# A decode layer with cached attention and a gated MLP: hand-set semaphores and a TensorE loop in place of the tile framework, and another order of the first loads

## The chip, the cores and the metric

The program runs on one core of a Trainium2 chip. Five engines work side by side: TensorE (PE in the profile, its weight loads PEld), VectorE (DVE), ScalarE (ACT), GpSimd (POOL) and SyncE (SP, which here issues nearly all transfers). Data moves from HBM into SBUF through DMA; products are accumulated in PSUM. The metric is the device time of one execution in microseconds, the median of the runs.

## The reference

One new token for each of 8 sequences. All arrays are float32; B = 8, D = 512, 32 query heads, 8 heads of K and V, 4096 cached positions, head size 128.

```python
xn = _layernorm(x, axis=-1)
# A: attention over the cache, four query heads share one K/V head
q = (xn @ wq).reshape(B, Sq, Hq, Dh)
scores = jnp.einsum("bhqd,bhkd->bhqk", q, k) * (Dh ** -0.5)
p = _softmax(scores, axis=-1)
o = jnp.einsum("bhqk,bhkd->bhqd", p, v)
s = o.reshape(B, Sq, Hq * Dh) @ wo
# B: gated MLP on the same xn, F = 1792, Fh = 896
z = _gelu(xn @ w_in)
z1 = z[..., :Fh]
z2 = _layernorm(z[..., Fh:], axis=-1)
g = w_sp * z2 + b_sp
return x + s * _silu((z1 * g) @ w_out)
```

The caches are 8 x 8 x 4096 x 128 floats each, 134 MB for K and as much for V; wq and wo have 8.39 MB each, w_in 3.67 MB and w_out 1.84 MB. Everything is read once.

## The kernel before

**Buffers.** SBUF holds three slots of 64 KB in each of 128 partitions (8.39 MB each): `pair[0]` and `pair[1]`, called slot0 and slot1, and `side`. The two slots of the pair take turns: for each head h, the first four batches' K goes to slot0, the last four's to slot1, then V in the same way. `side` holds the MLP weights at first and wo at the end.

**Order of the loads**, all on SyncE's queue in program order: `w_mlp` (w_in and five of the seven 128-row blocks of w_out, L77), three small transfers `w_low` (L82: the other two blocks of w_out, cut into pieces of a few rows and laid on 20, 16 and 12 partitions, with outer sizes 5, 4 and 3), `wq` into slot1 (L92), K of head 0 first half into slot0 and, when the projection has read wq, second half into slot1 (L348). Each later load waits until its slot has been read: V (L355) until `scores` has read K, the next head's K until `values` has read V. In the last head wo comes into `side` (L359), 12 of its 32 pieces before the last V half and the rest behind it in ever smaller transfers. x (L72) comes in two transfers on ScalarE's queue.

**The work.** A float32 product is two matrix instructions with a weight load each. After the layer norm of x (L148 to L156) the generator `mlp` runs up to its `yield` (z, gelu, second norm, L185 to L218); then `project_q` twice (L269 to L279), which makes the 32 queries; then the rest of `mlp`: transposes (L222, L232), the product with w_out in 20 pieces, 15 of which are `w_low` pieces (L246), and the gate. Then the 8 heads one after another: `spread_q` (L286) copies the head's queries into a padded tile, `scores` (L293) multiplies them with a K half, `softmax` (L298 to L325) takes maxima, exponentials and sums over both halves and transposes the probabilities, `values` (L335) multiplies them with V for one batch; VectorE masks and folds the result (L338, L340), and `combine` (L344) adds it into `po_ps` one batch later. At the end come the product with wo (L366, L374), the gate, the sum with x, and the store (L432).

**What sets the order.** The tile framework writes all heads out one after another, puts a semaphore wait into each instruction that needs one, and closes the program (L470) with waits of SyncE for all counts, a barrier of all engines, a clearing of the semaphores and a second barrier. At the start there is one barrier (L466), which belongs to the program frame.

Of the kernel before, what the change touches and what calls it, by code (L numbers as in the profile page):

```python
# [1 line left out]

# [9 lines left out]
AX = mybir.AxisListType  # L12

# [13 lines left out]
UNIT = 2 * G * 512  # L27
SLOT = HALF * UNIT
# [4 lines left out]
LOW_R = 4  # L33
MAIN = [0, 2, 4, 6, 5]


def rows_of(j, lo, hi, n):
    return [(j, r) for r in range(lo, hi, n)]


LOW = [(5, 0, 0, rows_of(1, 0, 80, 20) + rows_of(3, 0, 100, 20)), (4, 0, 9 * D, [(3, 100)]),
       (3, R, 0, rows_of(1, 80, P, 12) + [(3, 116)])]
LOW_COLS = 10 * D
HL_AT = [0, 9, 0]
HL_CH = 10
X_PARTS = 2
ALIGN = 200
XW = D + 64
E = 2
W = P // E  # L50


@with_exitstack
def tile_gqa_gmlp_decode(ctx: ExitStack, tc: tile.TileContext, x, kT, v, wq, wo,
                         w_mlp, lows, out):
    nc = tc.nc
    const = ctx.enter_context(tc.tile_pool(name="const", bufs=1))
    ring = ctx.enter_context(tc.tile_pool(name="ring", bufs=1))
    work = ctx.enter_context(tc.tile_pool(name="work", bufs=1))
    small = ctx.enter_context(tc.tile_pool(name="small", bufs=2))  # L60
    ps_fix = ctx.enter_context(tc.tile_pool(name="ps_fix", bufs=1, space=bass.MemoryType.PSUM))
    ps = ctx.enter_context(tc.tile_pool(name="ps", bufs=2, space=bass.MemoryType.PSUM))

    const.tile([P, ALIGN], F32, name="align")

    side = ring.tile([P, SLOT], F32, name="side")
    pair = [ring.tile([P, SLOT], F32, name=f"slot{i}") for i in range(2)]


    xs_sb = work.tile([B, XW], F32, name="x_sb", tag="p")  # L70
    for c in range(0, XW, XW // X_PARTS):
        nc.scalar.dma_start(xs_sb[:, c:c + XW // X_PARTS], x[:, c:c + XW // X_PARTS])  # L72
    x_sb = xs_sb[:, :D]

    mlp_slot = side
    n_in, n_mlp = NK * 2 * FH, NK * 2 * FH + len(MAIN) * D
    nc.sync.dma_start(mlp_slot[:, :n_mlp], w_mlp)  # L77
    w_in_sb = mlp_slot[:, :n_in].rearrange("p (k n) -> p k n", k=NK)
    low_sb = []
    for (e, p0, c0, chunks), w_low in zip(LOW, lows):  # L80
        t = mlp_slot[p0:p0 + e * LOW_R, n_mlp + c0:n_mlp + c0 + len(chunks) * D]
        nc.sync.dma_start(t, w_low[:, :LOW_R * len(chunks) * D].rearrange("e (i n) -> e i n", i=LOW_R))  # L82
        low_sb.append(t.rearrange("p (c d) -> p c d", d=D))
    w_out_sb = mlp_slot[:, n_in:n_mlp].rearrange("p (j d) -> p j d", d=D)
    spare = [n_mlp + LOW_COLS]

    def from_slot(rows, n):
        lo = spare[0]
        spare[0] = lo + n
        return mlp_slot[:rows, lo:lo + n]  # L90

    nc.sync.dma_start(pair[1], wq)  # L92
    wq_sb = pair[1].rearrange("p (k n) -> p k n", k=NK)


    ident = const.tile([P, P], F32, name="ident")
    make_identity(nc, ident)
    neg_half = const.tile([P, 1], F32, name="neg_half")
    nc.gpsimd.memset(neg_half, -0.5)
    ones = const.tile([1, P], F32, name="ones")  # L100
    nc.gpsimd.memset(ones, 1.0)
    xnT = const.tile([P, NK, R], F32, name="xnT")
    nc.gpsimd.memset(xnT, 0.0)
    qT = const.tile([P, HKV, B, REP], F32, name="qT")
    qz = const.tile([P, B * (R + REP)], F32, name="qz")
    nc.gpsimd.memset(qz, 0.0)
    same = const.tile([P, G, R], F32, name="same")
    nc.vector.tensor_reduce(same[:, 0, :], ident.rearrange("p (g r) -> p r g", g=G),
                            op=ALU.add, axis=AX.X)
    for g in range(1, G):  # L110
        nc.vector.tensor_copy(same[:, g, :], same[:, 0, :])
    same_all = same.rearrange("p g r -> p (g r)")
    diag = const.tile([P, G], F32, name="diag")
    nc.vector.tensor_reduce(diag, same[:, 0, :G * REP].rearrange("p (g r) -> p g r", g=G),
                            op=ALU.add, axis=AX.X)
    fold = const.tile([P, REP], F32, name="fold")
    nc.vector.tensor_reduce(fold, same[:, 0, :G * REP].rearrange("p (g r) -> p r g", g=G),
                            op=ALU.add, axis=AX.X)

    same8 = const.tile([P, (E - 1) * B + R], F32, name="same8")  # L120
    nc.gpsimd.memset(same8, 0.0)
    nc.vector.tensor_copy(same8[:, (E - 1) * B:E * B], same[:, 0, :B])
    oT_end = const.tile([P, HKV * REP - FOLDED, (E - 1) * B + R], F32, name="oT_end")
    nc.gpsimd.memset(oT_end, 0.0)
# [5 lines left out]
    sc = ps_fix.tile([P, 2, 512], F32, name="sc")  # L130
    o_ps = [ps_fix.tile([P, G, DH], F32, name=f"o_ps{i}") for i in range(2)]
    po_ps = ps_fix.tile([P, 2, B * REP], F32, name="po_ps")
    for t in o_ps:
        nc.vector.memset(t, 0.0)

    def scratch(shape, name):
        t = ps.tile([P, 512], F32, name="scr")
        n = 1
        for s in shape[1:]:
            n *= s  # L140
        return t[:shape[0], :n]


    st = small.tile([B, 6], F32, name="st")
    mv = small.tile([B, 2], F32, name="mv")
    rstd = small.tile([B, 2], F32, name="rstd")
    xn = work.tile([B, D], F32, name="xn", tag="pT")
    nc.vector.bn_stats(st, x_sb)  # L148
    nc.vector.bn_aggr(mv, st)
    nc.vector.tensor_scalar(rstd[:, 0:1], mv[:, 1:2], EPS, None, op0=ALU.add)  # L150
    nc.gpsimd.tensor_tensor(rstd[:, 1:2], rstd[:, 0:1], neg_half[:B, 0:1], op=ALU.pow)
    nc.vector.tensor_scalar(xn, x_sb, mv[:, 0:1], rstd[:, 1:2], op0=ALU.subtract, op1=ALU.mult)  # L152
    pt = scratch([P, NK * B], "xnT")
    for k in range(NK):
        nc.tensor.transpose(pt[:, k * B:(k + 1) * B], xn[:, k * P:(k + 1) * P], ident[:B, :B])  # L155
    nc.vector.tensor_copy(xnT[:, :, :B], pt.rearrange("p (k b) -> p k b", k=NK))  # L156

    gate = const.tile([P, W], F32, name="gate")
    xg = const.tile([P, W], F32, name="xg")
    wb = const.tile([P, 2], F32, name="wb")  # L160
    px = scratch([P, W + 2], "px")
    for i in range(E):
        for g in range(G):
            lo = g * P + i * W
            nc.tensor.matmul(px[R * g:R * (g + 1), :W], shift(same8, i)[:B], x_sb[:, lo:lo + W],
                             start=(i == 0), stop=(i == E - 1))
    nc.tensor.matmul(px[:, W:], ones, xs_sb[0:1, D:D + 2], start=True, stop=True)
    nc.vector.tensor_copy(xg, px[:, :W])
    nc.vector.tensor_copy(wb, px[:, W:])

    def mlp():
        zu = work.tile([P, 4, FQ], F32, name="zu", tag="p")
        z, u = zu[:, :2], zu[:, 2:]
        hy = work.tile([P, 2 * D], F32, name="hy", tag="pT")
        hT = hy[:, :2 * P].rearrange("p (a s) -> p a s", a=2)
        hL = from_slot(P, HL_CH * P).rearrange("p (a s) -> p a s", s=P)
        y_sb, e = zu[:, :2].rearrange("p a f -> p (a f)"), zu[:, 2, :W]
        pz = scratch([P, 2 * FQ], "pz")
        nc.vector.memset(pz, 0.0)
        for part in range(2):  # L180
            for k in range(NK):
                for g in range(G):
                    lo = g * FQ
                    n = min(FQ, FH - lo)
                    nc.tensor.matmul(pz[R * g:R * (g + 1), part * FQ:part * FQ + n], xnT[:, k, :],  # L185
                                     w_in_sb[:, k, part * FH + lo:part * FH + lo + n],
                                     start=(k == 0), stop=(k == NK - 1))
        zf, uf = z.rearrange("p a f -> p (a f)"), u.rearrange("p a f -> p (a f)")
        nc.vector.tensor_copy(zf, pz)
        nc.vector.tensor_mul(uf, zf, zf)  # L190
        nc.vector.tensor_scalar(uf, uf, 0.044715, 1.0, op0=ALU.mult, op1=ALU.add)
        nc.vector.tensor_mul(uf, uf, zf)
        nc.scalar.activation(uf, uf, AF.Tanh, scale=GELU_C)
        nc.vector.tensor_scalar(uf, uf, 1.0, 0.5, op0=ALU.add, op1=ALU.mult)
        nc.vector.tensor_mul(zf, uf, zf)

        def mean(src, name):
            part_sum = small.tile([P, 1], F32, name="part_sum")
            nc.vector.tensor_reduce(part_sum, src, op=ALU.add, axis=AX.X)  # L199
# [25 lines left out]
        for (ne, p0, _, chunks), c0, w_low in zip(LOW, HL_AT, low_sb):  # L225
            n = ne * LOW_R
            for lo in range(0, len(chunks), 4):
# [5 lines left out]
                for i, (j, r) in enumerate(some):  # L233
                    if i and rows[i] == rows[0]:
                        continue
# [146 lines left out]
    for _ in steps:  # L382
        pass
# [92 lines left out]
```

## Time and profile before

| | |
|---|---|
| median of 3 runs | 687.27 us (686.05 to 687.49) |
| span of the profiled execution | 685.0 us |
| instructions in the profile | 5902, of them 2699 matrix products and 2699 weight loads |
| TensorE, VectorE, ScalarE busy | 56%, 25%, 2% |
| read from HBM | 290.74 MB, 424 GB/s over the span |
| granted TensorE clock, mean | 0.76 |

The profile records one execution on its own; the span runs from its first to its last instruction. Of that execution no time but the span is given; the runs' times were taken without the profiler. In the groups, "idle before" is the time that the engine stood still ahead of such instructions, with what ended it. In the chain, each piece is followed back to what released it; a piece named DMA runs from the issue of a transfer to its landing, so it also holds the time in which the transfer stood in the queue.

### The profile page before, as it was taken

What the parts mean: (1) busy time and instruction counts of PE and PEld (TensorE: products, weight loads), DVE (VectorE), ACT (ScalarE), POOL (GpSimd) and SP (SyncE); (2) the same over time, 40 slices, a digit from 0 to 9 for tenths busy, and PEclk for the clock granted to TensorE, in tenths of its full rate; (3) what the DMA queues carried; (4) which work ended last, traced back from release to release, by engine and by line L of the source; (5) the groups of instructions that cost most, each with busy time, mean ns of one, the idle gap of its engine ahead of it and who ended that gap; (6) DMA issues with size and microseconds to landing.
All of it is one profiled execution on the core that took longest, in us unless ns stands there. A gap on an engine that the chain in (4) does not pass through costs nothing.

```text
span 685.0 us, 5902 instructions
## 1 busy us (share of the span) xinstructions
PE 381.6 (56%) x2699; PEld 116.7 (17%) x2699; DVE 170.5 (25%) x284; ACT 13.4 (2%) x27; POOL 2.8 (0%) x14
## 2 busy tenths in 40 slices
PE   2268745556764464555755355555754465655656
PEld 1112111111211021111211021111211121111212
DVE  2413023401430024401421024401431024401432
ACT  0100000000000000000000000000000000000000
POOL 1000000000000000000000000000000000000000
PEclk9768967777787677767778777776687667767799
DMA  9999999999999999999999999999999999999996
GB/s 400 436 432 396 368 429 448 445 440 430 429 426 429 426 440 441 429 430 440 433 436 426 432 430 429 430 444 437 429 426 436 433 429 433 444 441 429 405 425 262
DMA packets 6308, 291.14 MB, mean 425 GB/s; under 512 B 844, under 2 KB 860, under 8 KB 1388
## 3 DMA queue, kind: packets, MB, share of 16 engines
q1 hardware_dynamic: 6252, 290.75, 98.6%
q8 instruction: 21, 0.34, 0.2%
q10 hardware_dynamic: 32, 0.02, 0.0%
q14 instruction: 3, 0.02, 0.0%
HBM read 290.74 MB, written 0.03 MB: 424 GB/s over the span
## 4 chain that ended last, share of the span: by engine, by line
DMA 73%; PE 24%; DVE 1%; SPq 0%; issue 0%
DMA slot<-in_v 29%; DMA slot<-in_kT 29%; PE sc L293 11%; DMA side<-in_wo 10%; PE o_ps L335 9%; DMA slot<-in_wq 5%; PE scr L269 1%; PE sc L246 1%; PE po_ps L344 1%; SPq L82 0%; DVE o_sb L340 0%; PE scr L232 0%; DVE o_all L338 0%; DVE q_sb L272 0%; PE scr L275 0%
## 5 line engine op out<-in xcount | busy, mean ns | idle before, releaser
L293 PE MATMUL sc<-slot,qz 128*32 128x512 f32 x1024 | 145.9, 733 | 123.2 <-DMA slot<-in_kT 123.2
L335 PE MATMUL o_ps<-slot,pT 128*16 128x512 f32 x1024 | 155.5, 751 | 83.3 <-DMA slot<-in_v 83.3
L338 DVE TENSOR_TENSOR o_all<-o_ps,diag 128x512 f32<-128x512 f32 x64 | 44.3, 692 | 163.4 <-PE o_ps L335 163.4
L298 DVE TENSOR_REDUCE nm<-sc 128x1 f32<-128x1024 f32 x8 | 9.8, 1225 | 266.3 <-PE sc L293 266.3
L293 PEld LDWEIGHTS sc<-slot,qz 128*32 128x32 f32 x1024 | 35.5, 132 | 227.0 <-DMA slot<-in_kT 131.1
L340 DVE TENSOR_REDUCE o_sb<-o_all 128x128 f32<-128x512 f32 x64 | 67.8, 1060 | 2.2
L335 PEld LDWEIGHTS o_ps<-slot,pT 128*16 128x16 f32 x1024 | 30.6, 114 | 168.4 <-issue 113.0
L344 PE MATMUL po_ps<-fold,o_sb 128*128 128x4 f32 x128 | 24.6, 263 | 24.0 <-DVE o_sb L340 23.8
L344 PEld LDWEIGHTS po_ps<-fold,o_sb 128*128 128x128 f32 x128 | 19.0, 188 | 68.6 <-DVE o_sb L340 67.7
L324 PE MATMUL scr<-ident,p 128*128 128x128 f32 x64 | 14.8, 410 | 10.7 <-DVE p L319 10.7
L300 ACT ACTIVATE p<-sc,nm 128x1024 f32<-128x1024 f32 x8 | 8.9, 1114 | 554.6 <-DVE qz L286 460.1
L269 PE MATMUL scr<-slot,xnT 128*32 128x512 f32 x64 | 10.2, 798 | 9.5 <-DMA slot<-in_wq 9.5
L324 PEld LDWEIGHTS scr<-ident,p 128*128 128x128 f32 x64 | 11.9, 213 | 11.1 <-issue 11.1
L325 DVE COPY pT<-scr 128x512 f32<-128x512 f32 x16 | 11.1, 692 | 10.8 <-PE scr L324 10.7
L303 PE MATMUL scr<-ident,nm 128*1 128x128 f32 x8 | 2.2, 270 | 10.8 <-DVE nm L298 10.8
L316 PE MATMUL scr<-wl,same 128*128 128x1 f32 x16 | 3.4, 284 | 6.2 <-DVE wl L314 6.2
L185 PE MATMUL scr<-side,xnT 128*32 128x256 f32 (+1 forms) x64 | 4.9, 442 | 3.1 <-DMA side<-in_w_mlp 3.1
L155 PE MATMUL scr<-ident,xn 8*128 8x8 f32 x4 | 0.6, 254 | 10.5 <-DVE xn L152 10.5
L246 PE MATMUL sc<-side 20*32 20x512 f32 (+2 forms) x30 | 5.7, 650 | 0.8 <-DVE zu L249 0.8
L319 DVE TENSOR_SCALAR p<-p,w 128x1024 f32<-128x1024 f32 x8 | 6.0, 753 | 0.3
L366 PE MATMUL sc<-side,oT 128*8 128x512 f32 x48 | 5.7, 593 | 0.3 <-DMA side<-in_wo 0.3
L201 PE MATMUL scr<-part_sum,same 128*128 128x1 f32 x4 | 1.1, 348 | 8.3 <-DVE part_sum L199 8.3
(99 smaller groups left out, 75.1 us busy)
## 6 DMA issues: line engine op xcount, KB each, us to landing
slot<-in_v SPq DMA_DIRECT2D x2, 4096.0 KB, 32.2
side<-in_w_mlp SPq DMA_DIRECT2D x1, 4864.0 KB, 14.5
side<-in_wo SPq DMA_DIRECT2D x1, 3072.0 KB, 36.9
side<-in_wo SPq DMA_DIRECT2D x1, 2048.0 KB, 43.0
side<-in_wo SPq DMA_DIRECT2D x1, 1280.0 KB
side<-in_wo SPq DMA_DIRECT2D x1, 768.0 KB
side<-in_wo SPq DMA_DIRECT2D x1, 512.0 KB
side<-in_wo SPq DMA_DIRECT2D x2, 256.0 KB, 31.9
```

The lines of the kernel that those rows point to most:

```text
L246: nc.tensor.matmul(sc[R * g:R * (g + 1), bank, :], lhsT, rhs, start=(i < G), stop=(i + G >= len(part)))
L269: nc.tensor.matmul(pq[R * g:R * (g + 1), :], xnT[:, k, :], wq_sb[:, k, lo:lo + REP * DH], start=(k == 0), stop=(k == NK - 1))
L293: nc.tensor.matmul(sc[R * g:R * (g + 1), c, :], qz[:, b * R:(b + 1) * R], k_sb[:, i, c, g, :], start=(b == 0), stop=(b == B - 1))
L298: nc.vector.tensor_reduce(m, sc, op=ALU.max, axis=AX.XY, negate=True)
L300: nc.scalar.activation(p.rearrange("p j s -> p (j s)"), sc.rearrange("p c s -> p (c s)"), AF.Exp, bias=m, accum_out=l[:, h:h + 1])
L319: nc.vector.tensor_scalar(p, p, w, None, op0=ALU.mult)
L324: nc.tensor.transpose(t[:, j * P:(j + 1) * P], p[:, 4 * c + j, :], ident)
L325: nc.vector.tensor_copy(pT[:, :, 4 * c:4 * c + 4].rearrange("p b j (g r) -> p (j g) b r", g=G), t.rearrange("p (m b r) -> p m b r", b=B, r ...
L335: nc.tensor.matmul(of[R * c:R * c + G * REP, :], pT[:, b, j, :], v_unit[:, j], start=(j < G), stop=(j >= J - G))
L338: nc.vector.tensor_mul(o_all, o, diag[:, :, None].to_broadcast([P, G, DH]))
L340: nc.vector.tensor_reduce(o_sb, o_all.rearrange("p g d -> p d g"), op=ALU.add, axis=AX.X)
L344: nc.tensor.matmul(po[:, b * REP:(b + 1) * REP], o_sb, fold, start=True, stop=True)
```

## The change

- The tile framework goes. A class `Program` takes a list of operations with the names of what each reads and writes, works out who must wait for whom, and gives each engine one semaphore and each slot one of its own. Waits are instructions of their own. SBUF addresses and PSUM banks are set by hand: three scratch banks, one bank for `po`.
- TensorE's instructions of heads 0 to 6 are emitted once, in a loop of seven passes. To make all passes alike, a wait inside the loop takes the awaited count off the semaphore. The other engines' instructions are written out as before. Head 7 follows behind the loop.
- The first loads are, in this order: wq, the MLP weights with all seven blocks of w_out in one transfer over 128 partitions, K of head 0. The three `w_low` transfers, the transposes that served them and 13 of the 20 products with w_out go.
- Both projections come ahead of the whole MLP; `spread_q` of the next head comes behind the softmax of the head before. x comes in one transfer.
- The program ends when SyncE has seen the output land; it clears the semaphores before that wait. There is no barrier and no drain.

```diff
+    def wait(self, eng, waits):
+        for s, n, take in waits:
+            w = self.eng[eng].wait_ge(self.sem(s), n)
+            if take:
+                w.then_inc(self.sem(s), -n)
+
+    def put(self, o):
+        eng = self.eng[o.eng]
+        self.wait(o.eng, o.waits)
+        ins = o.emit(eng)
+        if o.inc:
+            ins.then_inc(self.sem(o.inc[0]), o.inc[1])
+
+    def build(self):
+        self.settle()
+        self.assign()
+        for e in ("SP", "ACT", "DVE", "POOL"):
+            for o in self.ops:
+                if o.eng == e:
+                    self.put(o)
+        pe = [o for o in self.ops if o.eng == "PE"]
+        turns = [[o for o in pe if o.where == h] for h in range(LOOPED)]
...
+        with self.nc.Fori(0, LOOPED, engines=[ET.PE]):
+            for o in turns[0]:
+                self.put(o)
+        for o in pe[first + sum(map(len, turns)):]:
+            self.put(o)
...
-    nc.sync.dma_start(mlp_slot[:, :n_mlp], w_mlp)
-    w_in_sb = mlp_slot[:, :n_in].rearrange("p (k n) -> p k n", k=NK)
-    low_sb = []
-    for (e, p0, c0, chunks), w_low in zip(LOW, lows):
-        t = mlp_slot[p0:p0 + e * LOW_R, n_mlp + c0:n_mlp + c0 + len(chunks) * D]
-        nc.sync.dma_start(t, w_low[:, :LOW_R * len(chunks) * D].rearrange("e (i n) -> e i n", i=LOW_R))
...
-    nc.sync.dma_start(pair[1], wq)
+    n_in, n_mlp = NK * 2 * FH, NK * 2 * FH + NB * D
+    pr.dma(lambda e: e.dma_start(xs_sb, x), "x_in", writes=["x"], eng="ACT")
+    load(pair[1], wq, "slot1", ["slot1"])
+    load(side[:, :n_mlp], w_mlp, "mlp_in", ["side"])
...
+    project_q(0)
+    project_q(1)
...
+    load_k(0, 0)
+    load_k(0, 1)
...
+        for j in range(NB):
+            g = j % G
+            mm(sc[R * g:R * (g + 1), 0, :], hT[:, j % 2, R * (j // 2):R * (j // 2 + 1)], w_out_sb[:, j, :],
+               j < G, j + G >= NB, ["hT", "side"], ["sc"])
...
+    mlp()
...
-    steps = mlp()
-    next(steps)
-    project_q(0)
-    project_q(1)
-    for _ in steps:
-        pass
+    spread_q(0)
     for h in range(HKV):
         last = h == HKV - 1
-        spread_q(h)
+        pr.where = h if h < LOOPED else None
         for half in range(2):
-            scores(half, load_k(h, half))
...
+            if h:
+                load_k(h, half)
+        scores(0)
+        load(pair[0], v[h, 0], "slot0", ["slot0"])
+        scores(1)
...
+            load(pair[1], v[h, 1], "slot1", ["slot1"])
+        softmax(h)
+        if not last:
+            spread_q(h + 1)
...
+    pr.dma(lambda e: e.dma_start(out, res), "out", reads=["res"], writes=["out"])
+    pr.build()
...
+    for s in (range(used[0], done.num), range(done.num + 1, used[-1] + 1)):
+        if len(s):
+            nc.sync.sem_clear(s)
+    nc.sync.wait_ge(done, 16).then_inc(done, -16)
```

More of the change, by code (lines that the diff above doesn't have):

```diff
@@ L128, in shift @@
         return t[:, lo:lo + R]
[L130 to L161, printed above, removed]
+    px = scr[1]
     for i in range(E):
@@ L192, in mlp @@
[L192 to L199, printed above, removed]
-            pm = scratch([P, 1], "pm")
-            nc.tensor.matmul(pm, same_all, part_sum, start=True, stop=True)
-            t = small.tile([P, 1], F32, name=name)
-            nc.vector.tensor_scalar(t, pm, 1.0 / FH, None, op0=ALU.mult)
-            return t
@@ new lines, in values, with combine @@
+        t, u = o_all[b % 2], o_sb[b % 2]
+        dve(lambda e: e.tensor_mul(t, o, diag[:, :, None].to_broadcast([P, G, DH])),
+            [f"o_ps{b % 2}", "diag"], [f"o_all{b % 2}"])
+        dve(lambda e: e.tensor_reduce(u, t.rearrange("p g d -> p d g"), op=ALU.add, axis=AX.X),
+            [f"o_all{b % 2}"], [f"o_sb{b % 2}"])
+    def combine(b):
+        mm(po[:, b * REP:(b + 1) * REP], o_sb[b % 2], fold, True, True, [f"o_sb{b % 2}", "fold"], ["po"])
+    wo_sb = side.rearrange("p (m d) -> p m d", d=D)
@@ L387, in tile_gqa_gmlp_decode @@
         for half in range(2):
-            scores(half, load_k(h, half))
-        pT = softmax(h)
-        po = po_ps[:, h % 2]
+            if h:
[3 more added lines that the diff above has]
+        scores(1)
+        if last:
+            load_wo(0, 0, WO_EARLY)
+            for c in range(2):
+                n = SLOT // 2
+                load(pair[1][:, c * n:(c + 1) * n], v[h, 1][:, c * n:(c + 1) * n], f"v_end{c}",
+                     [f"v_end{c}"] + ([] if c else ["slot1"]))
+            for i, (lo, hi) in enumerate(WO_LATE):
+                load_wo(1 + i, lo, hi)
+        else:
+            load(pair[1], v[h, 1], "slot1", ["slot1"])
@@ L402, in tile_gqa_gmlp_decode @@
             for i in range(HALF):
                 b = half * HALF + i
-                o_sb = values(b, pT, v_sb[:, i])
+                key = f"slot{half}" if not (last and half) else f"v_end{i // 2}"
+                values(b, v_sb[:, i], key)
                 if b > 0:
-                    combine(b - 1, o_prev, po)
-                o_prev = o_sb
+                    combine(b - 1)
         if last:
             folded_wo(WO_EARLY, WO_LATE[0][1])
-        combine(B - 1, o_prev, po)
+        combine(B - 1)
@@ L469 @@
     out = nc.dram_tensor("out_0", (P, W), F32, kind="ExternalOutput").ap()
[L470 to L472 removed]
+    program(nc, *args, out)
+    nc.compile()
     r = run(nc, [{f"in_{name}": a for name, a in arrays.items()}], core_ids=[0])
```

580 lines of the change are left out of this document (325 added, 255 removed).

## The prediction

> **What bounds the kernel now.** I begin with the page: the busy times, the slices of the span, the DMA queues and the shares of the chain.
>
> ```profile
> PE 381.6 (56%) x2699; PEld 116.7 (17%) x2699; DVE 170.5 (25%) x284; ACT 13.4 (2%) x27; POOL 2.8 (0%) x14
> ...
> DMA  9999999999999999999999999999999999999996
> GB/s 400 436 432 396 368 429 448 445 440 430 429 426 429 426 440 441 429 430 440 433 436 426 432 430 429 430 444 437 429 426 436 433 429 433 444 441 429 405 425 262
> ...
> q1 hardware_dynamic: 6252, 290.75, 98.6%
> q8 instruction: 21, 0.34, 0.2%
> ...
> DMA 73%; PE 24%; DVE 1%; SPq 0%; issue 0%
> ```
>
> The reader is to see that all 16 DMA engines are busy in nearly every slice. One queue, q1, moves 290.75 MB and holds the engines 98.6% of the span. TensorE is busy 56%, but its 24% of the chain is no proof that it limits anything, as the chain in order of time and the waits show.
>
> ```profile
> 3.71 35.42 DMA slot<-in_wq
> ...
> 65.87 8.58 PE sc L293 x64
> ...
> 74.47 24.01 DMA slot<-in_v
> ...
> 108.86 28.32 DMA slot<-in_kT
> ...
> 137.22 8.85 PE sc L293 x64
> ...
> 146.09 29.80 DMA slot<-in_v
> ...
> 681.70 0.04 issue
> 681.75 0.47 PE sc L374 x16
> ```
>
> ```profile
> PE sc L293 <- DMA slot<-in_kT: 123.2, 15, 10.9
> PE o_ps L335 <- DMA slot<-in_v: 83.3, 17, 7.2
> ```
>
> A slot holds 8.39 MB. A load issued at 108.86 takes 28.32 us, though its bytes need only 19.4 us (rate in the next rows): for 9 us it stands behind the load of the other slot. TensorE in its turn waits for K 8.2 us a time (123.2 / 15). So in the steady part neither delays nor gains of under about 8 us on TensorE, VectorE or SyncE reach the end; DMA time alone counts. Where does it run below its rate?
>
> ```profile
> 0.00:2.00 2.00, 0.00 (x0) 0.00 (x0) 0.97 (x2) 0.00 (x0) 1.43 (x12) 1.00 0.78 219
> 2.00:4.00 2.00, 0.00 (x0) 0.00 (x0) 0.00 (x0) 0.00 (x0) 0.23 (x1) 1.00 0.55 195
> 72.50:75.00 2.50, 1.90 (x20) 0.36 (x12) 0.00 (x0) 0.00 (x0) 0.00 (x0) 1.00 0.37 157
> 100.00:640.00 540.00, 300.13 (x1984) 88.67 (x1976) 131.22 (x195) 9.86 (x21) 0.00 (x0) 0.74 1.00 433
> 640.00:675.00 35.00, 25.30 (x170) 6.88 (x174) 12.53 (x15) 0.00 (x0) 0.00 (x0) 0.82 0.99 424
> 677.00:679.00 2.00, 1.14 (x9) 0.12 (x9) 0.71 (x2) 0.00 (x0) 0.00 (x0) 1.00 0.70 281
> 679.00:681.00 2.00, 1.63 (x101) 1.50 (x104) 0.18 (x1) 0.00 (x0) 0.00 (x0) 1.00 0.25 97
> 681.00:683.00 2.00, 1.00 (x59) 0.68 (x47) 0.45 (x2) 0.00 (x0) 0.00 (x0) 1.00 0.04 13
> ```
>
> These are windows; the last two numbers are DMA share and GB/s. The steady rate is 433 GB/s. At it all bytes take 290.75 / 433 = 671.5 us. The first 4 us move 0.83 MB, worth 1.9 us, so the start costs 2.1 us. The small pieces of wo cost 35 x (1 - 424/433) = 0.7 us. A program with full and equal engines would thus land its last weights at 671.5 + 2.1 + 0.7 = **674.3 us**; this one lands them at 681.70. The 7.4 us between are what the change can reach:
> - a hole at 72.5: 2.5 x 0.63 = 1.6 us on every engine;
> - a ragged end: shares of 0.70, 0.25 and 0.04 mean that an average engine idles 0.6 + 1.5 + 0.7 = 2.8 us before 681.70, waiting for the last one;
> - the rest, 3.0 us, in which the instruction fetches are part: 0.2% of 685 us on 16 engines is 21.9 us, 1.04 us for each of 21, 1.4 us an engine.
>
> **The change part by part.** *wq first, MLP weights second.* The rows are SyncE's issues (the second number runs to the end of the last of them) and the first network's work.
>
> ```profile
> 1.18 2.49 SPq L82 DMA_DIRECT2D side<-in_w_low  x3
> 4.18 47.03 SPq L348 DMA_DIRECT2D slot<-in_kT  x2
> 74.47 10.86 SPq L355 DMA_DIRECT2D slot<-in_v  x2
> ```
>
> ```profile
> 15.32 4.89 PE L185 MATMUL scr<-side,xnT 128*32 128x256 f32 x64 [3.15 <-DMA side<-in_w_mlp]
> 20.28 0.69 DVE L189 COPY zu<-scr 128x512 f32<-128x512 f32 x1 [7.78 <-PE scr L185]
> 31.58 0.42 DVE L218 TENSOR_TENSOR zu<-zu 128x256 f32<-128x256 f32 x1
> 61.51 2.92 PE L246 MATMUL sc<-side 12*32 12x512 f32 x10 [0.82 <-DVE zu L249]
> ```
>
> Today the second K half is issued at 51.2, and `scores` of the first half begins at 65.87, after the last w_out product; so V is issued only at 74.47, when some engines have run dry: the hole. After: wq lands near 2.1 + 19.4 = 21.5; the projection (from wq's landing at 39.13 to the second K issue, 51.2 - 39.1 = 12.1 us) ends at 33.6 and frees slot 1, so the second K half is queued 20 us before the first ends (21.5 + 5.51 MB in 12.7 + 19.4 = 53.6). The MLP starts at 34.2: 4.9 us of products, 11.7 us from L189 to the end of L218, then w_out. That part takes 51.2 to 65.87 today, 14.7 us; 15 transposes, their copies and 13 of 20 products leave it, and I put 7 us, between 3 and 14.7. `scores` starts near 58 and takes 8.6 us; V is issued near 67, 6 us ahead of the second K half's end at 73. Gain: 1.6 us. Its cover is those 6 us; extra waits eat 1 to 2 of them. If it is gone, the 1.6 us come back.
>
> *w_low gone, w_out whole.* Three issues (2.49 us on SyncE) go; a full queue hides them either way. Their 0.52 MB stay, now in rows over all partitions. Where they lie today counts: by 39.13, when wq lands, 13.9 MB have passed, which take 32.1 + 2.1 = 34.2 us, so some engines are 4.9 us late. Per engine of five, four and three, the transfers of 360, 32 and 120 KB (by the code) are 72 + 8 + 40 = 120 KB, at 433 / 16 = 27 GB/s 4.5 us: the same delay. [...] With one transfer the engines start level.
>
> *TensorE's loop.* These groups make one head's instructions:
>
> ```profile
> L293 PE MATMUL sc<-slot,qz 128*32 128x512 f32 x1024 | 145.9, 733 | 123.2 <-DMA slot<-in_kT 123.2
> L335 PE MATMUL o_ps<-slot,pT 128*16 128x512 f32 x1024 | 155.5, 751 | 83.3 <-DMA slot<-in_v 83.3
> L344 PE MATMUL po_ps<-fold,o_sb 128*128 128x4 f32 x128 | 24.6, 263 | 24.0 <-DVE o_sb L340 23.8
> L324 PE MATMUL scr<-ident,p 128*128 128x128 f32 x64 | 14.8, 410 | 10.7 <-DVE p L319 10.7
> ```
>
> That is 2240 / 8 = 280 products a head, each with a weight load: 560 instructions and a few more. TensorE's 5398 make 257 per fetch of 16 KB, so the fetches follow its stream: 2.2 a head, 15 in heads 0 to 6. If a body once fetched is kept, six heads' 13 fetches vanish and 8 stay: 13 x 1.04 / 16 = 0.85 us for an average engine, more for the latest. The branch itself is not in this trace: at least nothing, at most a fetch that waits for its place; each pass ends where TensorE waits 8.2 us for K anyway, and I take 0.
>
> With engines level and 8 fetches left, what does the last engine carry beyond 674.3? At least nothing; from today's side, today's average end 681.70 - 2.8 = 678.9, less 1.6 and 0.85, is 676.4, plus one fetch 1.04: 677.5. Between 674.3 and 677.5 I take **676.6**, nearer to the end that is built from today's rows.
>
> *Own semaphores.* Waits become instructions of their own. Nearest rows are those of the closing part, by the timeline, the line's own instructions and the DMA issues:
>
> ```profile
> 682.75 0.34 SPq L432 DMA_DIRECT2D out<-res  x1
> ```
>
> ```profile
> L470 SPq EVENT_SEMAPHORE  x8: 17/27/28, 683.2 to 685.0; - x8
> ```
>
> ```profile
> out<-res SPq DMA_DIRECT2D x1, 32.0 KB, 1.5
> ```
>
> A wait holds SyncE for 17 to 28 ns; with its gap I put 0.06 us. Behind TensorE's waits stand the next products, behind VectorE's the two operations of each batch; some ten waits a half head are 0.6 us against 8 of slack. Only those after the last weights count: three or four, 0.2 us (bounds 0 and 0.4). `spread_q` moves behind the softmax of the head before, one small copy on VectorE, hidden by the 4.9 us (83.3 / 17) that TensorE waits for V. x comes in one DMA and is needed at 21.5. The PSUM banks are fixed by hand, three for scratch and one for `po` in place of two; po's copy has a whole head's time, and I count nothing.
>
> *No closing barrier.* The output is issued at 681.70 + 1.05 = 682.75 and lands 1.5 later, near 684.25; the span ends at 685.0, so nearly 0.8 us go. After: 676.6 + 1.05 + 1.5 + 0.2 = 679.35. That is **5.65 us** less than 685.0. The profiled execution has no time of its own beside its span; the median 687.27 stands 2.3 us above it. The profile does not show what lies there and I leave it: **681.6 us**.
>
> **The rivals.** (1) *The loop does not keep its body*: each pass brings its 2.2 to 3 blocks again. Fetches stay at 21 to 29, and the end stays ragged: average 678.9 - 1.6 = 677.3, plus up to 8 x 1.04 / 16 = 0.5, plus a lag of the last engine of 1.5 to 2.8 us: 678.8 to 680.6, and with 2.75 us behind it and 2.3 around it 683.85 to 685.65, middle **684.7**. For it: a fetch came for every 257 instructions, all new. Against: nothing shows that executed blocks are dropped. [...]
>
> (2) *Refetched through the same engine, slower*: if a block always comes by the same DMA engine, a pass adds its fetch there each time. It decides from the point at which one engine's load is 685.0 - 2.75 - 674.3 = 8.0 us above the even one, 1.1 us a pass over seven. One fetch is 1.04 us; with half of that again for the transfer it interrupts, 1.5 x 7 = 10.9, on 674.3 + 1.0 of other lag: 686.2 + 2.75 = 688.95, 3.95 us more than 685.0: **691.2**. For it: even fetching on all engines is nowhere shown. Against: it needs rival 1 and a fixed engine together.
>
> (3) *The hole stays*: the MLP now stands between the projection and `scores`; if it ends 6 us later than worked out, 1.6 us come back: **683.2**.
>
> **How the numbers follow.** Forecast 0.55, rival 1 0.24, rival 2 0.13, rival 3 0.08. The forecast's own range is 679.8 (last weights near 674.8) to 682.8 (677.5, and 0.4 us of waits); rival 3 lies at its edge, rival 1 reaches 685.65. Leaving out rival 2 and the far ends gives 679.8 to 685.8. What a measurement of this kernel can tell from no change is 0.2%, 1.4 us: faster means below 685.9. Forecast and rival 3 are faster (0.63), and two thirds of rival 1 (0.16), whose upper end all but touches the bound; its rest, 0.08, with 0.02 of rival 2, is the same: 0.79, 0.10 and 0.11.
>
> **What would show it.** Right: share near 1.0 between 66 and 80; q8 with about 8 packets; an end where the share falls from 0.9 to 0 within some 2 us; the last weights at 675 to 678; nothing behind the output's landing. Wrong: q8 with 21 packets or more (rivals 1 and 2; a last engine later than 681 tells 2), a share under 0.5 before 80 (rival 3), or TensorE's waits for K near zero, which would mean that the loop eats its slack.

## The result, and the profile after

The changed kernel takes 678.81 us (median of four runs, 678.80 to 680.64) against 686.67 us for the kernel before on the same chip: ratio 0.9891, 95% interval [0.9875, 0.9906]. That is 7.9 us; on a second chip (below, after_again) it was 678.51 against 686.08, 7.6 us. The forecast was 5.65 us and 681.6 us with a range from 679.8; the time came out 1.0 us under the range. The direction held, and so did most of the mechanisms; several sizes did not, and one part of the gain the forecast did not have at all.

The page of the kernel after, the slices of DMA and the queues:

```profile
DMA  9999999999999999999999999999999999999997
GB/s 380 441 434 435 433 433 427 433 433 433 437 433 433 433 437 433 433 433 433 433 433 434 433 433 434 433 433 433 433 433 433 433 433 433 433 433 434 422 432 326
...
q1 hardware_dynamic: 6192, 290.75, 99.3%
q8 instruction: 7, 0.11, 0.1%
```

Two things differ from the page of before: the rate is 433 in almost every slice, where it wandered between 426 and 448 in the middle of the span, and q8, the queue of the instruction fetches, has 7 packets in place of 21. Its windows (the last two numbers are DMA share and GB/s):

```profile
72.50:75.00 2.50, 0.00 (x0) 0.00 (x0) 0.00 (x0) 0.00 (x0) 0.00 (x0) 0.50 1.03 446
100.00:640.00 540.00, 296.75 (x1988) 92.67 (x1984) 130.06 (x195) 9.14 (x21) 0.00 (x0) 0.75 1.00 434
673.00:675.00 2.00, 1.49 (x95) 1.20 (x83) 0.00 (x0) 0.00 (x0) 0.00 (x0) 1.00 0.37 136
675.00:677.00 2.00, 0.41 (x16) 0.25 (x16) 0.45 (x2) 0.00 (x0) 0.00 (x0) 1.00 0.06 14
```

The hole at 72.5 is gone (0.37 before). The steady rate is 434, not 433. The share falls from near 1 to 0.06 within two windows. The last pieces of the chain of waits, in order of time, and the store (start, length):

```profile
629.03 44.67 DMA side<-in_wo
673.71 0.14 issue
673.84 1.10 PE sc L256 x64
674.94 0.04 issue
674.99 0.47 PE sc L256 x16
```

```profile
675.99 0.35 SPq L541 DMA_DIRECT2D out<-res  x1
```

The last weights are in at 674.94 (681.70 before; forecast 676.6), the store is issued at 675.99, and the span ends at 677.5. This execution took 678.80 us in all, so 1.3 us lie around its span.

### The profile page after: what moved, and what is told of

It reads as the page before. It is cut to its first block, busy times and chain, and to the rows that moved or that the text cites. A ratio compares the mean times of both kernels' runs of the same rounds, so it can differ in the third digit from the quotient of the medians.

```text
span 677.5 us, 5837 instructions
## 1 busy us (share of the span) xinstructions
PE 371.5 (55%) x2658; PEld 118.5 (17%) x2658; DVE 167.3 (25%) x277; ACT 12.6 (2%) x27; POOL 2.8 (0%) x14
## 3 DMA queue, kind: packets, MB, share of 16 engines
q1 hardware_dynamic: 6192, 290.75, 99.3%
## 5 line engine op out<-in xcount | busy, mean ns | idle before, releaser
L256 PE MATMUL o_ps<-slot,pT 128*16 128x512 f32 x1024 | 153.3, 733 | 94.5 <-PEq L150 86.8
L256 PEld LDWEIGHTS sc<-slot,qz 128*32 128x32 f32 x1024 | 40.8, 132 | 227.9 <-issue 227.9
L421 DVE TENSOR_REDUCE m<-sc 128x1 f32<-128x1024 f32 x8 | 9.8, 1225 | 272.3 <-PE sc L256 272.3
L256 PEld LDWEIGHTS o_ps<-slot,pT 128*16 128x16 f32 x1024 | 29.0, 109 | 165.3 <-issue 156.0
L256 PE MATMUL po<-fold,o_sb 128*128 128x4 f32 x128 | 25.4, 269 | 12.3 <-PEq L150 12.1
L256 PEld LDWEIGHTS po<-fold,o_sb 128*128 128x128 f32 x128 | 20.1, 197 | 68.8 <-issue 63.4
L424 ACT ACTIVATE p<-sc,m 128x1024 f32<-128x1024 f32 x8 | 8.9, 1113 | 562.1 <-PE scr L259 562.1
L259 PEld LDWEIGHTS scr<-ident,p 128*128 128x128 f32 x66 | 12.0, 210 | 13.5 <-issue 9.7
L259 PE MATMUL scr<-ident,m 128*1 128x128 f32 x8 | 2.2, 269 | 11.4 <-PEq L150 10.1
L256 PEld LDWEIGHTS scr<-slot,xnT 128*32 128x32 f32 x64 | 2.5, 139 | 21.5 <-issue 21.5
L259 PE MATMUL scr<-ident,full 1*128 1x1 f32 x8 | 1.6, 201 | 5.6 <-PEq L150 5.0
```

The lines of the kernel that those rows point to most:

```text
L256: return pe(lambda e: e.matmul(out_, lhsT, rhs, start=start, stop=stop), reads, writes)
L259: return pe(lambda e: e.transpose(out_, in_, id_), reads, writes)
L421: dve(lambda e: e.tensor_reduce(m, sc, op=ALU.max, axis=AX.XY, negate=True), ["sc"], ["m"])
L424: act(lambda e: e.activation(p.rearrange("p j s -> p (j s)"), sc.rearrange("p c s -> p (c s)"), AF.Exp, bias=m, accum_out=l), ["sc", "m"], ...
```

## The experiments

Eighteen kernels ran, each timed in five rounds. All are the changed kernel with the edit shown, unless it says "kernel before". The column "before" is the kernel before on the same chip in the same batch; an amount "above the changed kernel" is against 678.51. By the kernel before the chips differ by up to 0.5 us (686.08 to 686.62), so such an amount is good to about that; ranges within one batch are tighter.

| kernel | us | before | ratio [95%] |
|---|---|---|---|
| after_again | 678.51 | 686.08 | 0.9889 [0.9873, 0.9904] |
| unrolled | 681.19 | 686.08 | 0.9925 [0.9911, 0.9938] |
| shift128 | 679.86 | 686.08 | 0.9906 [0.9891, 0.9922] |
| mlp_first | 678.80 | 686.08 | 0.9891 [0.9876, 0.9906] |
| skew | 683.98 | 686.62 | 0.9963 [0.9950, 0.9976] |
| unrolled_skew | 683.62 | 686.62 | 0.9959 [0.9946, 0.9972] |
| skew8 | 681.03 | 686.62 | 0.9920 [0.9907, 0.9934] |
| before_aligned | 685.27 | 686.62 | 0.9983 [0.9974, 0.9992] |
| level8 | 694.05 | 686.38 | 1.0107 [1.0091, 1.0122] |
| skew_big | 696.42 | 686.38 | 1.0139 [1.0123, 1.0155] |
| before_whole | 684.70 | 686.38 | 0.9969 [0.9957, 0.9982] |
| barrier | 679.19 | 686.38 | 0.9890 [0.9875, 0.9905] |
| rows112 | 692.01 | 686.33 | 1.0077 [1.0064, 1.0091] |
| extra_low | 683.13 | 686.33 | 0.9951 [0.9937, 0.9964] |
| extra_even | 679.87 | 686.33 | 0.9903 [0.9888, 0.9918] |
| undo_four | 683.63 | 686.33 | 0.9957 [0.9944, 0.9971] |
| shift64 | 680.05 | 686.39 | 0.9906 [0.9892, 0.9920] |
| align4096 | 678.64 | 686.39 | 0.9887 [0.9871, 0.9903] |

**The yardstick.**

> The changed kernel once more, as the yardstick for the other kernels on the same chip. Expected: 678.8 to 680.6 us, q8 with 6 to 8 packets, the last weights landed within 0.5 us of 674.94.

678.41 to 678.95 us, 7 packets on q8, last weights at 674.55. As expected.

**The loop.**

```diff
-        with self.nc.Fori(0, LOOPED, engines=[ET.PE]):
-            for o in turns[0]:
+        for turn in turns:
+            for o in turn:
                 self.put(o)
```

> Heads 0 to 6 written out on TensorE in place of the loop; waits, semaphores, loads and places are those of the changed kernel. Theory A (the loop saves instruction fetches, and these delay the last DMA engine): q8 goes back to about 21 packets, the last weights land 1.5 to 3 us later (676.4 to 678), the end becomes ragged again, and the time is 1.5 to 3 us above the changed kernel. Rival B (the fetches are hidden, the gain is from the level start alone): 21 packets, but the time within 0.5 us of the changed kernel.

2.7 us above the changed kernel: theory A. Page and windows of the unrolled kernel:

```profile
q8 instruction: 21, 0.34, 0.2%
```

```profile
671.00:673.00 2.00, 2.00 (x18) 0.52 (x14) 0.98 (x2) 0.00 (x0) 0.00 (x0) 1.00 0.91 368
673.00:675.00 2.00, 2.00 (x22) 0.66 (x18) 0.99 (x2) 0.00 (x0) 0.00 (x0) 1.00 0.53 215
675.00:677.00 2.00, 2.00 (x127) 1.77 (x123) 0.69 (x1) 0.00 (x0) 0.00 (x0) 1.00 0.29 111
```

The fetches are back, and with them the ragged end. The trace counts the landing of each load of K, V or wo sixteen times, and I take each count for one of the page's 16 DMA engines; of the last load the first and the last count lie 4.5 us apart here (672.74 and 677.24) and 1.7 us apart in the changed kernel (673.24 and 674.94). So the first engine is no later for the fetches, and the last is 2.3 us later. In the sixteen landings of each load one sees how that comes: behind a fetch one of them comes some 1.5 us later, and behind the next fetch it is another. In the unrolled kernel the ninth fetch of q8 (at 294 us) is the first to hit an engine a second time, and the seventeenth (at 590 us) the first to hit one a third time: the landings look like eight engines hit in turn. In the last load four are about 4.3 to 4.5 us behind the first, four about 2.9 to 3.3, seven less than 0.5. The one left, 1.7 us behind, was hit by two fetches of 8 KB of another queue, q14, at 56 and 407 us. In the changed kernel six engines were hit once each by the fetches of q8 ahead of the end, and a seventh by the two of q14. The trace does not number the engines; this is read from the landing times alone.

**The slots' address.**

```diff
-SLOT_AT = 1536
+SLOT_AT = 1664
```

> The three slots start 128 bytes further on (SLOT_AT 1664 in place of 1536), as far from a multiple of 256 as those of the kernel before. Theory A (the address of the slot sets the rate): a load in the steady part takes 19.35 us as in the kernel before, in place of 19.32, and the time is 1.0 us above the changed kernel. Rival B (the address does not matter, the 0.03 us are the missing fetches): time within 0.4 us of the changed kernel.

1.35 us above the changed kernel, with ranges that don't meet (679.80 to 679.96 against 678.41 to 678.95): theory A, a little larger. The first products of a K half show the period, as they start when it has landed; after_again and then shift128, first half of heads 1 and 7, 24 loads apart:

```profile
133.38 3.64 PE L256 MATMUL sc<-slot,qz 128*32 128x512 f32 x16 [6.46 <-PEq L150]
...
597.11 3.32 PE L256 MATMUL sc<-slot,qz 128*32 128x512 f32 x16 [6.23 <-PEq L150]
```

```profile
133.65 2.79 PE L256 MATMUL sc<-slot,qz 128*32 128x512 f32 x12 [6.00 <-PEq L150]
...
598.25 2.79 PE L256 MATMUL sc<-slot,qz 128*32 128x512 f32 x12 [6.20 <-PEq L150]
```

463.73 / 24 = 19.32 us a load against 464.60 / 24 = 19.36. All bytes are 290.75 / 8.39 = 34.7 such loads: 34.7 x 0.036 = 1.25 us. The same the other way, in the kernel before, whose slots start at 9344 = 36.5 x 256:

```diff
-ALIGN = 200
+ALIGN = 232
```

> The kernel before with 128 bytes more ahead of its slots (ALIGN 232 in place of 200), so that they start at a multiple of 256; nothing else. Theory A (the address sets the rate): a load in the steady part takes 19.32 us in place of 19.35, and the time is 1.0 to 1.35 us below the kernel before (684.7 to 685.1). Rival B (in the kernel before the last engine is late for other reasons, which hide it): within 0.4 us of the kernel before.

1.35 us below the kernel before. Two more starts:

```diff
-SLOT_AT = 1536
+SLOT_AT = 1600   # shift64
+SLOT_AT = 4096   # align4096
```

> The three slots start 64 bytes further on (SLOT_AT 1600). Theory A (every start that isn't a multiple of 256 costs the same): 1.35 us above the changed kernel (679.9). Theory B (the cost grows as the start goes against a smaller unit, 64 bytes): more than 1.6 us above it. Rival C (it was not the start but what shift128 pushed elsewhere): within 0.4 us of the changed kernel.

> The three slots start at 4096, a multiple of 4096, in place of 1536, a multiple of 512. Theory A (a multiple of 256 is enough): within 0.4 us of the changed kernel. Rival B (a coarser unit brings more): 0.5 us or more below it, a version faster than both.

shift64 is 1.5 us above the changed kernel (theory A), align4096 0.1 us above it (theory A, no gain). With the slots at 9472 (kernel before), 1536 or 4096 (changed kernel), all multiples of 256, the time was some 1.2 to 1.5 us less than in the same kernel with 9344, 1664 or 1600. Why, nothing here shows.

**The order of the loads.**

```diff
-    load(pair[1], wq, "slot1", ["slot1"])
     load(side[:, :n_mlp], w_mlp, "mlp_in", ["side"])
+    load(pair[1], wq, "slot1", ["slot1"])
...
-    mlp()
+    steps = mlp()
+    next(steps)
+    project_q(0)
+    project_q(1)
+    load_k(0, 0)
+    load_k(0, 1)
+    for _ in steps:
+        pass
```

> MLP weights first, then wq, the second K half queued only after wq has been used and the rest of the MLP behind the projection, as in the kernel before; w_out stays whole, the loop and the semaphores stay. Theory A (the order of the loads removed the hole): the share falls below 0.5 in a window of some 2 us near 70 to 73, as V is issued too late, and the time is 1.0 to 1.6 us above the changed kernel. Rival B (the hole came from the 13 extra products and the transposes of the three small transfers): no hole, time within 0.4 us of the changed kernel.

0.3 us above the changed kernel with ranges that overlap: rival B. Its SyncE timeline and window:

```profile
46.70 0.33 SPq L262 DMA_DIRECT2D slot<-in_kT  x1
65.76 20.21 SPq L262 DMA_DIRECT2D slot<-in_v  x2
```

```profile
72.50:75.00 2.50, 0.00 (x0) 0.00 (x0) 0.00 (x0) 0.00 (x0) 0.00 (x0) 0.50 0.97 419
```

The second K half is queued nearly as late as before the change (at 46.70, against 50.88 there and 34.31 in the changed kernel), yet V is issued at 65.76, not 74.47, and there is no hole. V is even issued earlier than in the changed kernel (67.50). So the new order is not needed to close it; what is left of the change there is the whole w_out, with the MLP's shorter end and the level start.

**w_out in one transfer**, alone, in the kernel before:

```diff
-MAIN = [0, 2, 4, 6, 5]
+MAIN = [0, 1, 2, 3, 4, 5, 6]
-LOW = [(5, 0, 0, rows_of(1, 0, 80, 20) + ...
-LOW_COLS = 10 * D
-HL_AT = [0, 9, 0]
+LOW = []
+LOW_COLS = 0
+HL_AT = []
```

> The kernel before with w_out whole in the one transfer of the MLP weights: the three transfers of w_low, their 13 extra products, their transposes and copies are gone; the tile framework, the order (MLP weights first, first part of the MLP, projection, rest of the MLP), the written-out heads, the slots' address and the closing part stay. Theory A (w_low made both the uneven start and the hole): share near 1.0 between 72.5 and 75; by the account 678.5 + 2.6 (loop) + 1.35 (address) + 0.8 (closing) the time is 683.3, 2.8 us below the kernel before. Rival B (the order made the hole, or the fetches hide the uneven start): less than 1.2 us below it.

1.7 us below the kernel before: between the two. The hole is closed in the old order as well: wq's last count comes at 36.8 us, not 39.1, and V is issued at 64.47, not 74.47. Windows of before_whole:

```profile
72.50:75.00 2.50, 0.00 (x0) 0.00 (x0) 0.00 (x0) 0.00 (x0) 0.00 (x0) 0.50 0.97 419
...
675.00:677.00 2.00, 1.09 (x43) 0.52 (x39) 0.69 (x1) 0.00 (x0) 0.00 (x0) 1.00 0.49 181
677.00:679.00 2.00, 1.71 (x108) 1.39 (x97) 0.00 (x0) 0.00 (x0) 0.00 (x0) 1.00 0.16 62
```

but with 21 fetches the end stays ragged (first and last count of the last load at 674.0 and 679.1).

**What the shape of w_low costs.** The first trial cut the last two blocks of w_out (shown shortened), the second did it in the written-out kernel, the third with other sizes:

```diff
+TAIL = [(5, 18), (4, 2), (3, 10)]   # skew8: [(8, 10), (16, 3)]
...
-    load(side[:, :n_mlp], w_mlp, "mlp_in", ["side"])
+    load(side[:, :n_mlp - 2 * D], w_mlp, "mlp_in", ["side"])
+    for i, (e, r) in enumerate(TAIL):
+        n = e * r
+        load(side[p0:p0 + n, n_mlp - 2 * D:n_mlp],
+             tails[i][:, :r * 2 * D].rearrange("e (r d) -> e r d", r=r), f"tail{i}", [f"tail{i}"])
+        p0 += n
```

> The last two blocks of w_out (0.52 MB) come in three transfers with outer sizes 5, 4 and 3, as w_low did before; nothing else changes. Engine by engine that is 120 KB for the first three, 80 and 72 KB for the next two and none for eleven, in place of 32 KB each: the first three are 88 KB or 3.3 us late from the start, eleven are 1.2 us early. Theory A (the level start is a large part of the gain): the lateness stays to the end, the last weights land at 673.2 + 3.3 = 676.5, or at 678.0 if one of the seven fetches (1.5 us) falls on one of the three, and the time is 1.6 to 3.1 us above the changed kernel. Rival B (the engines even out on the way, as the loads wait for each other): within 0.4 us of the changed kernel.

> Heads 0 to 6 written out and the three transfers of outer sizes 5, 4 and 3 together. Theory A1 (the fetches come through other engines than the first five): the two kinds of lateness fall on different engines and don't add; the last weights land near 676.5, the time is about 0.8 us below that of the unrolled kernel (680.4 against 681.2). Theory A2 (they come through the same engines): they add, the last weights land at 679.6 to 681 and the time is 2.3 to 3.6 us above the unrolled kernel (683.5 to 684.8).

> The last two blocks of w_out in two transfers of outer sizes 8 (80 rows) and 16 (48 rows): the first eight engines get 52 KB, the other eight 12 KB, in place of 32 KB each; 0.74 us later and 0.74 us earlier from the start. Theory A1 (the fetches come through the last eight engines): the engines are evened out, the last weights land 0.7 us earlier (674.2), and the time is 0.7 us below the changed kernel: a version faster than both. Theory A2 (they come through the first eight, or through engines of both halves): 0.7 us above the changed kernel.

All three missed: 5.5, 5.1 and 2.5 us above the changed kernel. The trial was spoiled by itself: with its pieces of 4 KB the transfers beside and behind them were slower, too. In the windows of the changed kernel and of skew

```profile
22.00:52.00 30.00, 17.08 (x146) 6.80 (x150) 9.84 (x28) 0.63 (x1) 0.57 (x1) 0.89 1.04 450
```

```profile
22.00:52.00 30.00, 17.93 (x153) 7.05 (x156) 9.85 (x28) 0.63 (x1) 0.57 (x1) 0.86 1.04 398
```

the engines are as busy, but move (450 - 398) x 30 / 434 = 3.6 us less. Whether the size of the pieces does that or the partitions on which they lie, no run tells. Only one thing can be read from these trials: unrolled_skew is not above skew, so the lateness by shape and the lateness by fetches don't add. The landings of unrolled_skew's last load agree: the first three landings lie within 0.4 us, and the other thirteen come 2.4 us or more behind the first, which is five engines late by shape and eight others by fetches. I then cut larger pieces (21.5 KB), and it grew worse:

```diff
+P0, CUT = 112, 5376
+TAIL = [(8, 2)]   # skew_big: [(3, 4), (4, 1)]
...
+    load(side[:P0, :n_mlp], w_mlp[:P0], "mlp_in", ["side"])
+    load(side[P0:, :CUT], w_mlp[P0:, :CUT], "mlp_cut", ["mlp_cut"])
...
```

> Rows 112 to 127 of the second half of the MLP weights' columns (0.34 MB) come in one transfer of outer size 8, two rows of 21.5 KB for each of the first eight engines, in place of one row for each of sixteen: the first eight start 0.8 us late, the other eight 0.8 us early, without the 4 KB pieces of skew8. Theory A1 (the fetches fall mostly on the other eight): last weights at 673.24 + 0.95 = 674.2, time 0.7 us below the changed kernel (677.8). Theory A2 (they fall on the first eight, or on both): last weights at 675.8, time 0.8 us above it (679.3). Rival B (what made skew8 2.5 us slower was the uneven start itself, not its 4 KB pieces): 681.

> The skew once more with pieces of 21.5 KB: of rows 112 to 127 of the second half of the MLP weights' columns, twelve go by outer size 3 and four by outer size 4; the first three engines get 107 KB, the fourth 21.5, twelve none. The first three are 3.2 us late, twelve 0.8 us early. Theory A (lateness at the start stays to the end; the rest of skew's loss came from its 4 KB pieces): the last weights land at 676.4 (678 if a fetch falls on one of the three), the time is 1.5 to 3 us above the changed kernel (680.0 to 681.5), and the 64 KB packets behind the pieces take about 2.4 us. Rival B (the lateness costs more than itself): 684 as in skew.

15.5 and 17.9 us above, against all theories stated. Whether the uneven sizes or the 112 rows did it, rows112 tells, in which by the code each of sixteen engines gets eight rows, as in the changed kernel:

```diff
-    load(side[:, :n_mlp], w_mlp, "mlp_in", ["side"])
+    load(side[:112, :n_mlp], w_mlp[:112], "mlp_in", ["side"])
+    load(side[112:, :n_mlp], w_mlp[112:], "mlp_end", ["side_end"])
```

> The MLP weights in two transfers by rows, 0 to 111 and 112 to 127, both over sixteen engines (seven rows and one row for each): every engine gets the same bytes as in the changed kernel, only other partitions. [...]

13.5 us above, with even sizes: q1 has sixteen packets more for one load more (6208 against 6192), as many as the landing counts of a load over all engines. Its window:

```profile
22.00:52.00 30.00, 13.41 (x106) 4.77 (x109) 2.35 (x10) 0.00 (x0) 0.00 (x0) 0.75 0.97 240
```

Engines with a share of 0.97 at 240 GB/s in place of 450: (450 - 240) x 30 / 434 = 14.5 us, the whole loss. In the trace the rows of 43,008 bytes take 3.05 us on average, against 1.59 in the changed kernel. So the cause, as far as it was measured, is the cut at 112 rows; why the rows then take so long, nothing here shows.

The clean trial loads pieces in the manner of w_low, on top of everything else:

```diff
+    # extra_even
+    load(side[:, n_mlp:n_mlp + 2 * D], more[0], "more0", ["more0"])
+    # extra_low
+    for i, (e, p0, c0, n) in enumerate([(5, 0, 0, 9), (4, 0, 9 * D, 1), (3, R, 0, 10)]):
+        load(side[p0:p0 + e * 4, n_mlp + c0:n_mlp + c0 + n * D],
+             more[i][:, :4 * n * D].rearrange("e (i n) -> e i n", i=4), f"more{i}", [f"more{i}"])
```

> The changed kernel with 0.52 MB of zeros loaded besides, as one transfer of 4 KB a partition over all 128; nothing reads them. All theories: the bytes alone, 0.52 MB at 433 GB/s, 1.2 us above the changed kernel (679.7).

> The changed kernel with 0.52 MB of zeros loaded besides into unused columns behind w_out, by three transfers in the shapes of w_low (outer sizes 5, 4 and 3; rows of 18, 2 and 20 KB); nothing reads them. It is to be read against extra_even, which loads as many bytes evenly. Theory A (the shape of w_low makes the first engines late and the lateness stays to the end): 1.5 to 3.5 us above extra_even (681.2 to 683.2). Rival B (the shape costs nothing; what the whole w_out brings is the work that it saves): within 0.5 us of extra_even.

679.87 and 683.13: the even bytes cost 1.4 us, the uneven ones another 3.3. But extra_low is larger than I wrote: its third transfer has ten blocks where w_low has five, 240 KB in place of 120, so that 0.65 MB came, not 0.52, and the first three engines got 160 KB, not 120. By the first engines' bytes, 40 KB at 434 / 16 = 27 GB/s, that is 1.5 us too much; the shape of w_low itself would cost 3.3 - 1.5 = 1.8 us, an estimate that was not run. The mechanism stands out all the same, in windows of extra_low:

```profile
673.00:675.00 2.00, 1.97 (x22) 0.63 (x18) 1.33 (x3) 0.00 (x0) 0.00 (x0) 1.00 0.76 304
675.00:677.00 2.00, 1.42 (x44) 0.64 (x39) 0.78 (x2) 0.00 (x0) 0.00 (x0) 1.00 0.32 131
677.00:679.00 2.00, 1.56 (x108) 1.41 (x96) 0.00 (x0) 0.00 (x0) 0.00 (x0) 1.00 0.22 79
```

0.22 of 16 engines is three and a half: three engines, and for part of the time a fourth, work alone for 2 us, 600 us after the transfer that made them late. In the landings their lateness is 6.5 us at first and 6.3 in the load that ends at 138 us; in the next it is 5.3, which nothing here explains, and from there to the end it stays between 5.1 and 5.4. So most of it is never evened out.

**The closing part, and the sum.**

```diff
     nc.sync.wait_ge(done, 16).then_inc(done, -16)
+    nc.all_engine_barrier()
```

> The changed kernel with a barrier of all engines behind SyncE's wait for the output. Theory A (the closing part was worth what lay behind the output's landing, 0.8 us): the time is 0.5 to 1 us above the changed kernel, all of it behind the landing. Rival B (the end of the program brings a wait of that kind anyway): within 0.2 us of the changed kernel.

```diff
# undo_four: the edits of unrolled, shift128, mlp_first and barrier together
```

> Four parts undone together in the changed kernel: heads written out, slots 128 bytes further on, the order of the kernel before, a barrier at the end; w_out stays whole. Theory A (the parts add up): 678.5 + 2.7 + 1.35 + 0.3 + 0.7 = 683.5. Rival B (they don't add, or the tile framework cost something of its own besides): if it comes to 684.7, as the kernel before with w_out whole, the parts cost more together; if it stays at 683.5 or below, some 1.2 us are left for the framework's own waits and tiles.

barrier is 0.7 us above the changed kernel (its chip was 0.3 us slower by the kernel before). undo_four came to 683.63, where the sum of its parts gave 683.5: they add up, within the 0.3 us by which the chips differ. It and before_whole then differ in the framework with its allocation, in the place of `spread_q` and in x's two transfers, and by 1.1 us (0.9 in the two profiled executions). The place is the close; the stores of undo_four and of before_whole, by SyncE's timeline:

```profile
680.17 0.35 SPq L543 DMA_DIRECT2D out<-res  x1
```

```profile
680.16 0.35 SPq L431 DMA_DIRECT2D out<-res  x1
```

Both issue the store at the same time, but one span ends at 681.9 and the other at 682.9. From the store's issue to the end of the whole execution it is 678.80 - 675.99 = 2.8 us in the changed kernel, 683.73 - 680.17 = 3.6 with the barrier, and 684.63 - 680.16 = 4.5 with the framework's close. In before_aligned, which has that close as well, it is 685.12 - 681.04 = 4.1; why before_whole takes 0.4 us more there, nothing shows. So the close was worth 1.3 to 1.7 us, and where it is taken as 1.3, w_out in one transfer is worth 2.1 in place of 1.7.

## Why the prediction was right or wrong

| part | forecast | measured |
|---|---|---|
| hole at 72.5, w_low to whole w_out | 1.6 and a share of the ragged end | 1.7 in all (before_whole), 2.1 ahead of the close |
| loop | 0.85, "more for the latest" | 2.7 (unrolled) |
| address of the slots | not named | 1.35 (shift128, before_aligned) |
| order of the loads | held to be what closes the hole | 0.3 or none (mlp_first) |
| closing part | 0.8, less 0.2 of waits | 1.7 (before_whole against the changed kernel, from the store on), 1.3 by before_aligned |
| sum | 5.65 | 7.75 (1.7 + 2.7 + 1.35 + 0.3 + 1.7), against 7.6 to 7.9 |

*What bounds it*: right. DMA time alone set the end of the loads, and the gain or loss of each part but the close is to be found at the last engine.

*The step that failed*: two terms of the sum were mis-sized, and between them they make up nearly all of the 2.8 us from 681.6 to 678.8. The first is the last engine, "Between 674.3 and 677.5 I take **676.6**": it was in at 674.94, 1.7 us earlier. The second is the 2.3 us around the span, which became 1.3. It is the second that put the time under the range: 674.94 lies inside the bounds for the last weights, and the measured span of 677.5 with 2.3 around it would have given 679.8, the range's lower edge.

*The last engine.* In the landings of the last load the average engine ends at 679.4 in the profile of before, at 676.2 in before_whole and at 674.0 in the changed kernel. So w_out in one transfer took 3.1 us off the average engine (up to some 0.5 less, as the profiled execution of before is a long one: a span of 685.0, where most later ones have 684.1 to 684.8). The forecast took off 1.6, for the hole; what more the hole and the uneven start cost the engines was in the average of 678.9, "built from today's rows", and went with them. How the two share the 3.1, no run separates. The other 2.2 us are the address and the fetches, by the prices above 1.25 (against nothing) and 14 x 1.5 / 16 = 1.3 (against 0.85). The steady rate of 433 was carried over as fixed, though 0.036 us a load were the address of the slots, which moves with the framework's allocation and which I read over in the diff. With it the even floor is 674.3 - 1.25 = 673.05, and one delay by a fetch of 1.5 us puts the last engine at 674.55, near the 674.94 measured. Bounds with a slow rate in both ends leave out the case in which the rate changes.

*The 2.3 us around the span*, left as they were, became 1.3. In kernels with a closing barrier they are 1.7 to 1.8 (before_aligned 685.12 - 683.3, before_whole 684.63 - 682.9, undo_four 683.73 - 681.9), so 0.5 us of this is gain from the close, outside of the span, where no view shows it. The other 0.5 was an error of the sum: a span of 685.0 belongs to about 686.8 (686.79 and 686.85 in two later runs of the kernel before), not to the median of 687.27 that I set beside it. The 0.8 us that the close was to bring inside the span came: from the store to the span's end it is 2.25 us before and 1.5 after.

*The loop*: right in kind; 8 fetches were forecast, 7 came. Rivals 1 and 2 needed a refetch in each pass and fell with that: the body has 560 matrix instructions and more, or 2.2 fetches at 257 a fetch, it ran seven times, and the whole program has 7 fetches, of which one, at 359 us, falls between 108 and 624. From what length on a body would be fetched again, no run shows. The size was off threefold, as I priced a fetch by its own 1.04 us on an average engine. What counts is how often one engine is hit, three times 1.5 against once; of that only "more for the latest" was said, without a size.

*The order*: the times were right. Forecast were a start of `scores` near 58 and V near 67; the timeline has

```profile
58.68 3.94 PE L256 MATMUL sc<-slot,qz 128*32 128x512 f32 x20 [2.13 <-PEq L150]
```

```profile
67.50 17.56 SPq L262 DMA_DIRECT2D slot<-in_v  x2
```

and rival 3 fell. But the credit was wrong, and that the hole went as forecast was luck: before_whole and mlp_first lack it without the new order. The whole w_out, with its 13 products and 15 transposes fewer and its level start, was enough.

*The level start*: right that a lateness of some engines stays to the end (5.1 to 5.4 us in extra_low) and that w_low makes such a lateness: in the trace of before its three transfers land in five, four and three counts (the last of each at 17.90, 18.22 and 19.77 us, against 15.19 for w_mlp), and the sixteen counts of wq behind them lie between 33.66 and 39.13; in the changed kernel those of wq lie 0.5 us apart. But the forecast counted two losses, the hole of 1.6 us and the uneven start, where there was largely one: in the trace of before the sixteen counts of a load lie 5.5 us apart at 53 us, and 2.5 us apart at 96, behind the hole, in which the engines ahead stood still and the late ones caught up. So w_low costs 1.7 to 2.1 with the hole (before_whole) and, by the estimate above, 1.8 without it (extra_low).

*Waits of their own*: the 0.2 us do not show; from the last weights to the store's issue it is 1.05 us before and after (681.70 to 682.75, 674.94 to 675.99).

## What to carry to other kernels

Where all DMA engines are full, as here (share 1.00 from 100 to 640 us), look at the last engine, which here set the time (its last weights at 674.94 in the changed kernel, at 677.24 in unrolled): ask of each transfer and of each instruction fetch which engines it falls on, since most of a lateness, once there, stayed for 600 us (in extra_low 5.1 to 5.4 of 6.5 us). Look through a rewrite for what it moves without saying so: here the start of the buffers was worth half of what the loop was. Undo one part at a time and then all together; when the parts add up to the whole, as here within some 0.3 us, no large part has been overlooked.

## What the runs showed of the hardware

- With the slots at 1536 a load of 8.39 MB took 19.32 us (after_again), at 1664 19.36 (shift128), at 9344 19.35 (before). With the start at a multiple of 256 bytes (1536, 4096, 9472) a kernel took some 1.2 to 1.5 us less than the same one with another start (1600, 1664, 9344).
- With a load over 112 and 16 partitions in place of 128, its window of 30 us moved 240 GB/s in place of 450, with a DMA share of 0.97 (rows112); that cost 13.5 us for 5.5 MB.
- With 0.52 MB in rows of 4 KB, over neighbouring partitions by five, four and three engines, the loads beside and behind them were slower (skew, 398 GB/s in place of 450 for 30 us, 3.6 us); with rows of 18 and 20 KB in extra_low they were not (445 GB/s in the same window). These lie on other partitions as well, so the size of the rows is not shown to be the cause.
- An instruction fetch of 16 KB set one DMA engine back by some 1.5 us, not by its own 0.9 to 1.1 (0.93 to 1.11 in the trace of before), and successive fetches on q8 hit different engines, eight in turn by the landings (unrolled).
- The kernels that close with a barrier took 1.7 to 1.8 us besides the profiled span (before_whole, before_aligned, undo_four, barrier), the others 1.3 to 1.4: about 0.5 us behind the last instruction that a profile shows, besides what the barrier takes in the span.

None of these kernels is faster than the changed one.
